# One core, grouped-query decode attention with a gated block: V of a step and K of the next in one 8 MiB transfer

## The chip, the core and the metric

The kernel runs on one core of a Trainium2 chip. TensorE (PE) multiplies matrices, VectorE (DVE) and ScalarE (ACT) work on tiles, SyncE (SP) issues the large transfers, and 16 DMA engines move them from the chip's main memory into the on-chip memory of 128 partitions. The metric is the device time of one execution in microseconds (us). Before the change it is 378.41 us, the median of 3 runs (378.18 to 378.69).

## What is computed

```python
def _A_ref(x, k_cache, v_cache, wq, wo):
    B, Sq, D = x.shape                     # 2, 1, 448
    Hq, Dh = 16, 256                       # Hkv = 8, Sk = 4096
    q = (x @ wq).reshape(B, Sq, Hq, Dh).transpose(0, 2, 1, 3)
    k = jnp.repeat(k_cache, 2, axis=1)
    v = jnp.repeat(v_cache, 2, axis=1)
    scores = jnp.einsum("bhqd,bhkd->bhqk", q, k) * (Dh ** -0.5)
    p = _softmax(scores, axis=-1)
    o = jnp.einsum("bhqk,bhkd->bhqd", p, v)
    return o.transpose(0, 2, 1, 3).reshape(B, Sq, Hq * Dh) @ wo
...
x = A_x
xn = _layernorm(x, axis=-1)
s = _A_ref(xn, A_k_cache, A_v_cache, A_wq, A_wo)
g = _silu(((xn @ w_gate) * (xn @ w_up)) @ w_down)      # F = 1792
return x + s * g
```

Everything is float32. For each of 2 batches and 8 key/value heads the caches hold 4096 positions by 256 values: 4 MiB of K and 4 MiB of V. With 16 such pairs and the weights, 158.5 MB are read once.

## The kernel before

**Steps.** The main loop (L279) runs over i = 0 to 13, one step for each pair of a key/value head g and a batch b (`g, b = divmod(i, 2)`); the last two steps, 14 and 15, stand behind it. A step has three parts. `scores(i)` (L195) multiplies q with K of the step: 16 matmuls of 128x512 in float32, which PE carries out as 32, into two PSUM banks, each followed by a maximum over the row on DVE (L206). `softmax` (L210) joins the maxima of the 128 partitions (a transposition on PE, L213, a maximum on DVE, L215, a matmul with a 1x1 one, L218, that turns the row back into a column, and a scaling, L219), takes exponentials on ACT (L224), transposes them on DVE (L226), and adds up and inverts the sums (L228 to L230). `values(i)` (L233) multiplies the exponentials with V: again 16 matmuls, 32 on PE, into the bank `o`, which ACT scales into `ob` (L286).

**Other work, placed by hand between the steps.** `query(0)` and `query(1)` (L151) make q of the first and the last four heads; `ffn_in` (L170) and `ffn_out` (L182) the gated block, behind steps 1 and 2; `combine` and `turn` (L240, L255) put the outputs of eight or six steps into the shape of a stationary operand; `project` (L261) multiplies them with parts of wo into the bank `wide`, `spread` (L162) brings `wide` into the bank `acc`, and `project_last` (L267) adds the last eight heads to `acc`. Two DVE operations (L338, L339) and a store (L340) follow.

**Order.** The order on every engine is that of the program. The large loads are listed by `plan` (L52) in the order in which they are to come, and `issue` (L55) gives the next ones to SP, which waits, where it must, until the buffer is free. All go through one pool, `ring`, of 5 buffers of 32 KB in each partition. The list is wq0, K0, V0, K1, V1, wg, wu, K2, V2, wd, K3, V3, and so on, with wq1 ahead of K6, wo0 ahead of K9, and at the end wo1, K14, K15, V14, V15 (in three pieces), wo2 (in four). The first five are issued at the start (L83). A K or V block is one transfer of 128 rows of 32 KB.

**The end.** Behind the loop come `combine` and `turn` of six steps, `project` of wo1, `spread`, then scores and softmax of step 14, scores and softmax of step 15 (L312 to L315), V of 14, half of V of 15, the joining of step 14, the other half of V of 15, and the last heads.

Of the kernel before, what the change touches and what calls it, by code (L numbers as in the profile page):

```python
# [8 lines left out]
F32 = mybir.dt.float32  # L9
# [4 lines left out]
B, D = 2, 448  # L14
HKV, REP, SK, DH = 8, 2, 4096, 256
# [5 lines left out]
FC = F // NT  # L21
KB = 16
ROW = 8192
SL = D // NT
NC = HKV * 4
EARLY = 16
LATE = 24
THIRD = [24, 25, 28, 29, 30, 31, 26, 27]
EPS = 1e-5

# [5 lines left out]
@with_exitstack  # L36
def gated_decode_block(ctx: ExitStack, tc: tile.TileContext, x, xo, kt, v, wq, wo, wg, wu, wd, out):
    nc = tc.nc
    ring = ctx.enter_context(tc.tile_pool(name="ring", bufs=5))
    const = ctx.enter_context(tc.tile_pool(name="const", bufs=1))  # L40
# [4 lines left out]
    def bank(name="s", bufs=3):  # L45
        return psum.tile([128, 512], F32, name=name, bufs=bufs)


    loaded = {}
    todo = []  # L50

    def plan(name, src, cuts=None):  # L52
        todo.append((name, src, cuts or [0, src.shape[1]]))

    def issue(n=1):  # L55
        for name, src, cuts in todo[:n]:
            t = loaded[name] = ring.tile([128, ROW], F32, name="ring", align_bytes=512)
            for lo, hi in zip(cuts, cuts[1:]):
                nc.sync.dma_start(t[:, lo:hi], src[:, lo:hi])  # L59
        del todo[:n]  # L60

    N = HKV * B
    LAST = N - B
    plan("wq0", wq[0])
    for i in range(LAST):
        if i == 2:
            plan("wg", wg)
            plan("wu", wu)
        if i == 3:
            plan("wd", wd)  # L70
        if i == 6:
            plan("wq1", wq[1])
        if i == 9:
            plan("wo0", wo[:, :EARLY * D])
        plan(f"k{i}", kt[i % B, i // B])
        plan(f"v{i}", v[i % B, i // B])
    plan("wo1", wo[:, EARLY * D:LATE * D])
    plan(f"k{LAST}", kt[0, HKV - 1])
    plan(f"k{LAST + 1}", kt[1, HKV - 1])
    plan(f"v{LAST}", v[0, HKV - 1])  # L80
    plan(f"v{LAST + 1}", v[1, HKV - 1], [0, 4096, 7168, 8192])
    plan("wo2", wo[:, LATE * D:], [0, 2 * D, 6 * D, 7 * D, 8 * D])
    issue(5)  # L83

# [76 lines left out]

    def spread(ps, dst, start, stop):  # L162

        t = work.tile([128, D], F32, name="h")
        nc.scalar.copy(t, ps[:, :D])
        for n in range(NT):
            nc.tensor.matmul(dst[W * n:W * (n + 1), :SL], add_tiles.rearrange("p b j -> p (b j)"),
                             t[:, n * SL:(n + 1) * SL], start=start, stop=stop)

    def ffn_in():  # L170
        pp = []
        for w in ("wg", "wu"):
            ps = bank()
            rows(ps, loaded[w], FC)
            pp.append(ps)
        g = work.tile([128, FC], F32, name="h")
        nc.scalar.copy(g, pp[0][:, :FC])
        h = work.tile([128, FC], F32, name="h")
        nc.vector.tensor_mul(h, pp[1][:, :FC], g)
        nc.vector.transpose(hT.rearrange("p i m -> p (i m)"), h)  # L180

    def ffn_out():  # L182
        ps = bank()
        for i in range(14):
# [25 lines left out]
    def softmax(ss, m):  # L210
        nc.vector.tensor_max(m[:, 2:3], m[:, 0:1], m[:, 1:2])  # L211
        sm = bank("sm", 1)
        nc.tensor.transpose(sm[:1, :128], m[:, 2:3], ident)  # L213
        mx = work.tile([1, NT, W], F32, name="mx")
        nc.vector.tensor_reduce(  # L215
            mx, sm[:1, None, :128].rearrange("p o (c j) -> p o j c", c=NT).to_broadcast([1, NT, W, NT]),
            axis=AX.X, op=OP.max)
        nc.tensor.matmul(sm[:, 128:129], mx.rearrange("p c j -> p (c j)"), one, start=True, stop=True)  # L218
        nc.vector.tensor_scalar(m[:, 3:4], sm[:, 128:129], -1.0 / 16, None, op0=OP.mult)  # L219
# [53 lines left out]
    query(0)  # L273
    issue()
    ob = work.tile([128, 8, 512], F32, name="ob", bufs=1)
    oT0 = const.tile([128, 4, 2, REP, W], F32)
    oT1 = const.tile([128, 3, 2, REP, W], F32)
    oT2 = const.tile([128, 1, 2, REP, W], F32)
    for i in range(LAST):  # L279
        g, b = divmod(i, B)  # L280
        ss = scores(i)
        issue()
        p = softmax(*ss)
        o = bank("o", 1)
        values(i, p[0], o)
        nc.scalar.activation(ob[:, b * 4 + g if g < 4 else b * 3 + g - 4], o, AF.Copy, scale=p[1])  # L286
# [92 lines left out]
```

## Time and profile before

| what | value |
|---|---|
| median of 3 runs | 378.41 us |
| the profiled execution | 378.55 us |
| its span | 376.4 us |
| PE, DVE, ACT busy | 222.5, 72.7, 39.8 us |
| bytes read | 158.54 MB |
| mean granted TensorE clock | 0.77 |

How to read it: the span runs from the first to the last instruction of the profiled execution, and the 2.15 us around it belong to the run's time as well. Busy time is the time in which an engine executes something; for PE, which works in a pipeline, it is rough. The profile's page lists the span in 40 slices, the DMA queues, the chain of work that ended last, groups of instructions (line, engine, operation, shapes and count, then busy us and mean ns, then the idle time ahead of them and what ended it) and the DMA issues with their sizes and the time from issue to landing. Windows give the busy time of each engine in a stretch (PE, PE's weight loads, DVE, ACT, GpSimd), then the granted clock, the DMA share and GB/s. Timeline rows give start and duration in us, engine, line, operation and count.

### The profile page before, as it was taken

What the parts mean: (1) busy time and instruction counts of PE and PEld (TensorE: products, weight loads), DVE (VectorE), ACT (ScalarE), POOL (GpSimd) and SP (SyncE); (2) the same over time, 40 slices, a digit from 0 to 9 for tenths busy, and PEclk for the clock granted to TensorE, in tenths of its full rate; (3) what the DMA queues carried; (4) which work ended last, traced back from release to release, by engine and by line L of the source; (5) the groups of instructions that cost most, each with busy time, mean ns of one, the idle gap of its engine ahead of it and who ended that gap; (6) DMA issues with size and microseconds to landing.
All of it is one profiled execution on the core that took longest, in us unless ns stands there. A gap on an engine that the chain in (4) does not pass through costs nothing.

```text
span 376.4 us, 3397 instructions
## 1 busy us (share of the span) xinstructions
PE 222.5 (59%) x1456; PEld 65.6 (17%) x1456; DVE 72.7 (19%) x176; ACT 39.8 (11%) x87; POOL 1.2 (0%) x7
## 2 busy tenths in 40 slices
PE   0665556566376566646566655664656475574775
PEld 0112111112122111101121111121112121111122
DVE  3013030121021402102121310222112210304211
ACT  1001011001202200200102110011101010111011
POOL 1000000000000000000000000000000000000000
PEclk9966869766965877687886978669686966699669
DMA  8999999999999999999999999999999999999993
GB/s 333 437 439 416 435 430 438 428 429 444 425 434 439 435 420 436 438 435 432 420 439 437 432 424 432 442 437 421 427 442 435 435 423 428 435 428 445 414 417 132
DMA packets 6530, 158.75 MB, mean 422 GB/s; under 512 B 754, under 2 KB 1012, under 8 KB 1396
## 3 DMA queue, kind: packets, MB, share of 16 engines
q1 hardware_dynamic: 6496, 158.54, 98.0%
q8 instruction: 11, 0.18, 0.2%
q14 instruction: 3, 0.02, 0.0%
q10 hardware_dynamic: 20, 0.01, 0.0%
HBM read 158.54 MB, written 0.00 MB: 421 GB/s over the span
## 4 chain that ended last, share of the span: by engine, by line
DMA 76%; PE 18%; DVE 3%; issue 1%; ACT 1%; SPq 0%; ACTq 0%
DMA ring<-kt 55%; DMA ring<-v 12%; DMA ring<-wd 9%; PE s L205 8%; PE o L237 6%; DVE pT L226 1%; PE wide L237 1%; PE s L186 1%; PE cb L246 1%; DVE m L206 1%; DVE mx L215 1%; PE sm L229 0%; PE acc L270 0%; SPq L59 0%; PE sm L218 0%
## 5 line engine op out<-in xcount | busy, mean ns | idle before, releaser
L205 PE MATMUL s<-ring,qT 128*32 128x512 f32 x512 | 82.0, 799 | 50.9 <-DMA ring<-kt 50.9
L237 PE MATMUL o<-ring,pT 128*32 128x512 f32 x480 | 82.4, 849 | 1.6 <-DMA ring<-v 1.6
L206 DVE TENSOR_REDUCE m<-s 128x1 f32<-128x512 f32 x32 | 22.1, 692 | 177.5 <-PE s L205 177.5
L224 ACT ACTIVATE p<-s,m 128x512 f32<-128x512 f32 x32 | 21.7, 682 | 197.1 <-DVE m L219 197.1
L205 PEld LDWEIGHTS s<-ring,qT 128*32 128x32 f32 x512 | 20.5, 141 | 110.3 <-issue 78.5
L229 PE MATMUL sm<-su,add_head 128*128 128x1 f32 x32 | 9.4, 362 | 42.4 <-DVE su L228 42.4
L237 PEld LDWEIGHTS o<-ring,pT 128*32 128x32 f32 x480 | 18.9, 149 | 51.5 <-issue 50.9
L226 DVE STREAM_TRANSPOSE pT<-p 128x512 f32<-128x512 f32 x32 | 22.1, 711 | 15.7 <-ACT p L224 15.7
L143 PE MATMUL s<-ring,xnT 128*32 128x512 f32 (+1 forms) x96 | 14.3, 746 | 12.3 <-DMA ring<-wq 7.7
L286 ACT ACTIVATE ob<-o,su 128x512 f32<-128x512 f32 x14 | 9.6, 687 | 98.8 <-PE o L237 98.8
L229 PEld LDWEIGHTS sm<-su,add_head 128*128 128x128 f32 x32 | 8.0, 311 | 43.8 <-DVE su L228 43.8
L213 PE MATMUL sm<-ident,m 128*1 128x128 f32 x16 | 4.3, 270 | 17.3 <-DVE m L211 17.3
L218 PE MATMUL sm<-one,mx 1*128 1x1 f32 x32 | 6.8, 279 | 12.3 <-DVE mx L215 12.3
L215 DVE TENSOR_REDUCE mx<-sm 1x128 f32<-1x512 f32 x16 | 10.9, 679 | 7.0 <-PE sm L213 7.0
L264 PE MATMUL wide<-ring,oT 128*32 128x448 f32 x48 | 6.6, 698 | 4.1 <-DMA ring<-wo 3.3
L218 PEld LDWEIGHTS sm<-one,mx 1*128 1x128 f32 x32 | 5.4, 211 | 15.8 <-DVE mx L215 15.8
L143 PEld LDWEIGHTS s<-ring,xnT 128*32 128x32 f32 x96 | 3.6, 132 | 21.0 <-issue 17.0
L213 PEld LDWEIGHTS sm<-ident,m 128*1 128x1 f32 x16 | 1.3, 79 | 32.4 <-issue 26.6
L256 DVE STREAM_TRANSPOSE oT<-cb 128x256 f32<-128x256 f32 (+2 forms) x6 | 1.9, 347 | 25.5 <-PE cb L246 25.5
L224 ACT ACTIVATION_READ_ACCUMULATOR p<-s,m 128x1 f32 x32 | 6.3, 196 | 0.0
L155 DVE STREAM_TRANSPOSE qT<-s 128x256 f32<-128x256 f32 x4 | 1.6, 428 | 21.6 <-PE s L146 21.6
L246 PE MATMUL cb<-ob,add_blocks 128*32 128x64 f32 (+2 forms) x64 | 4.2, 384 | 2.3 <-ACT ob L286 1.6
(57 smaller groups left out, 47.0 us busy)
## 6 DMA issues: line engine op xcount, KB each, us to landing
ring<-kt SPq DMA_DIRECT2D x16, 4096.0 KB, 40.4
ring<-v SPq DMA_DIRECT2D x15, 4096.0 KB, 41.8
ring<-wq SPq DMA_DIRECT2D x2, 3584.0 KB, 11.3
ring<-wo SPq DMA_DIRECT2D x1, 3584.0 KB, 40.7
ring<-wg SPq DMA_DIRECT2D x1, 3136.0 KB
ring<-wu SPq DMA_DIRECT2D x1, 3136.0 KB
ring<-wd SPq DMA_DIRECT2D x1, 3136.0 KB, 34.5
ring<-v SPq DMA_DIRECT2D x1, 2048.0 KB
```

What stands on the lines that cost most here:

```text
L143: nc.tensor.matmul(ps[W * c:W * (c + 1), :n], xnT[:, k, :], block(NT * k + c), start=k == 0, stop=False)
L205: nc.tensor.matmul(s[W * c:W * (c + 1), :], q[:, d], k[:, h, d, c, :], start=d == 0, stop=d == 1)
L206: nc.vector.tensor_reduce(m[:, h:h + 1], s, axis=AX.X, op=OP.max)
L215: nc.vector.tensor_reduce(mx, sm[:1, None, :128].rearrange("p o (c j) -> p o j c", c=NT).to_broadcast([1, NT, W, NT]), axis=AX.X, op=OP.max)
L218: nc.tensor.matmul(sm[:, 128:129], mx.rearrange("p c j -> p (c j)"), one, start=True, stop=True)
L224: nc.scalar.activation(p, ss[h], AF.Exp, bias=m[:, 3:4], scale=1.0 / 16, accum_out=su[:, h:h + 1])
L226: nc.vector.transpose(t.rearrange("p i m -> p (i m)"), p)
L229: nc.tensor.matmul(sm[:, 130:131], add_head.rearrange("p a r j -> p (a r j)"), su[:, 2:3], start=True, stop=True)
L237: nc.tensor.matmul(o[W * t:W * (t + 1), :], pT[h].rearrange("p i m -> p (i m)")[:, at:at + 2 * W:2], loaded[f"v{i}"][:, e * 512:(e + 1) * ...
L246: nc.tensor.matmul(cb[W * c:W * (c + 1), :n * 64], add_blocks[:, e].rearrange("p r j -> p (r j)"), src[:, :n, e, :, c, :], start=e == 0, s ...
L264: nc.tensor.matmul(wide[W * t:W * (t + 1), :D], heads(oT, i, first), loaded[name][:, (i - base) * D:(i - base + 1) * D], start=i < NT, sto ...
L286: nc.scalar.activation(ob[:, b * 4 + g if g < 4 else b * 3 + g - 4], o, AF.Copy, scale=p[1])
```

## The change

K of step 0 is loaded by itself (`first`); from then on V of step i and K of step i + 1 lie side by side in one array, `vk[i]`, with 64 KB a row, and are loaded as one transfer of 8 MiB. The pool `ring` has 2 buffers of 64 KB a partition instead of 5 of 32 KB. The weights wq0, wg, wu, wd, wq1, wo0, wo1 and wo2 go one after the other through a pool of their own, `slot`, with one buffer of 28 KB. K15 and V14 share a buffer, loaded in two pieces; V15 comes in three pieces, as before.

So the order of the work changes. Step i of the loop is now values(i), then scores(i + 1), then softmax of i + 1. The next 8 MiB can be issued when both V of i and K of i + 1 have been used. In steps 0 and 1 the issue stands behind `gate_in` and `up_in` (`late`), because the weights to come need the slot. `ffn_in` is split into these two, in steps 0 and 1. `softmax` is split into its first part and `over`, the adding up and inverting. The matmul with a one, L218, becomes a transposition. At the end come scores of 14 (in the loop), softmax of 14 without `over`, scores of 15, `over` of 14, `project` of wo1, softmax of 15, V of 14, `spread`, `over` of 15, and V of 15; what follows is as before.

```diff
@@ -34,9 +35,10 @@
 
 
 @with_exitstack
-def gated_decode_block(ctx: ExitStack, tc: tile.TileContext, x, xo, kt, v, wq, wo, wg, wu, wd, out):
+def gated_decode_block(ctx: ExitStack, tc: tile.TileContext, x, xo, first, vk, last0, last1, wq, wo, wg, wu, wd, out):
     nc = tc.nc
-    ring = ctx.enter_context(tc.tile_pool(name="ring", bufs=5))
+    ring = ctx.enter_context(tc.tile_pool(name="ring", bufs=2))
+    slot = ctx.enter_context(tc.tile_pool(name="slot", bufs=1))
     const = ctx.enter_context(tc.tile_pool(name="const", bufs=1))
     work = ctx.enter_context(tc.tile_pool(name="work", bufs=2))
     psum = ctx.enter_context(tc.tile_pool(name="psum", bufs=1, space=bass.MemoryType.PSUM))
@@ -46,41 +48,39 @@
         return psum.tile([128, 512], F32, name=name, bufs=bufs)
 
 
+
+    N = HKV * B
+    LAST = N - B
     loaded = {}
     todo = []
 
-    def plan(name, src, cuts=None):
-        todo.append((name, src, cuts or [0, src.shape[1]]))
-
     def issue(n=1):
-        for name, src, cuts in todo[:n]:
-            t = loaded[name] = ring.tile([128, ROW], F32, name="ring", align_bytes=512)
+        for names, src, cuts in todo[:n]:
+            if len(names) == 1 and names[0].startswith("w"):
+                t = loaded[names[0]] = slot.tile([128, PART], F32, name="slot", align_bytes=512)
+            else:
+                t = ring.tile([128, 2 * ROW], F32, name="ring", align_bytes=512)
+                for i, name in enumerate(names):
+                    loaded[name] = t[:, i * ROW:(i + 1) * ROW]
             for lo, hi in zip(cuts, cuts[1:]):
                 nc.sync.dma_start(t[:, lo:hi], src[:, lo:hi])
         del todo[:n]
 
-    N = HKV * B
-    LAST = N - B
+    def plan(names, src, cuts=None):
+        todo.append((names.split(), src, cuts or [0, src.shape[1]]))
+
     plan("wq0", wq[0])
+    plan("k0", first)
+    weights = {0: ("wg", wg), 1: ("wu", wu), 2: ("wd", wd), 4: ("wq1", wq[1]), 8: ("wo0", wo[:, :EARLY * D]),
+               12: ("wo1", wo[:, EARLY * D:LATE * D])}
     for i in range(LAST):
-        if i == 2:
-            plan("wg", wg)
-            plan("wu", wu)
-        if i == 3:
-            plan("wd", wd)
-        if i == 6:
-            plan("wq1", wq[1])
-        if i == 9:
-            plan("wo0", wo[:, :EARLY * D])
-        plan(f"k{i}", kt[i % B, i // B])
-        plan(f"v{i}", v[i % B, i // B])
-    plan("wo1", wo[:, EARLY * D:LATE * D])
-    plan(f"k{LAST}", kt[0, HKV - 1])
-    plan(f"k{LAST + 1}", kt[1, HKV - 1])
-    plan(f"v{LAST}", v[0, HKV - 1])
-    plan(f"v{LAST + 1}", v[1, HKV - 1], [0, 4096, 7168, 8192])
+        plan(f"v{i} k{i + 1}", vk[i])
+        if i in weights:
+            plan(*weights[i])
+    plan(f"k{LAST + 1} v{LAST}", last0, [0, ROW, 2 * ROW])
+    plan(f"v{LAST + 1}", last1, [0, 4096, 7168, 8192])
     plan("wo2", wo[:, LATE * D:], [0, 2 * D, 6 * D, 7 * D, 8 * D])
-    issue(5)
+    issue(3)
 
     x2 = const.tile([B, D], F32)
     nc.scalar.dma_start(x2, x)
@@ -159,24 +159,29 @@
     gate = const.tile([128, SL], F32)
     hT = const.tile([128, 14, W], F32)
 
-    def spread(ps, dst, start, stop):
-
+
+    def lift(ps):
         t = work.tile([128, D], F32, name="h")
         nc.scalar.copy(t, ps[:, :D])
+        return t
+
+    def spread(t, dst, start, stop):
         for n in range(NT):
             nc.tensor.matmul(dst[W * n:W * (n + 1), :SL], add_tiles.rearrange("p b j -> p (b j)"),
                              t[:, n * SL:(n + 1) * SL], start=start, stop=stop)
 
-    def ffn_in():
-        pp = []
-        for w in ("wg", "wu"):
-            ps = bank()
-            rows(ps, loaded[w], FC)
-            pp.append(ps)
-        g = work.tile([128, FC], F32, name="h")
-        nc.scalar.copy(g, pp[0][:, :FC])
+    def gate_in():
+        ps = bank()
+        rows(ps, loaded["wg"], FC)
+        g = const.tile([128, FC], F32)
+        nc.scalar.copy(g, ps[:, :FC])
+        return g
+
+    def up_in(g):
+        ps = bank()
+        rows(ps, loaded["wu"], FC)
         h = work.tile([128, FC], F32, name="h")
-        nc.vector.tensor_mul(h, pp[1][:, :FC], g)
+        nc.vector.tensor_mul(h, ps[:, :FC], g)
         nc.vector.transpose(hT.rearrange("p i m -> p (i m)"), h)
 
     def ffn_out():
@@ -186,7 +191,7 @@
             nc.tensor.matmul(ps[W * t:W * (t + 1), :D], hT[:, i], loaded["wd"][:, i * D:(i + 1) * D],
                              start=i < NT, stop=i >= 14 - NT)
         y = bank()
-        spread(ps, y, True, True)
+        spread(lift(ps), y, True, True)
         e = const.tile([128, SL], F32)
         nc.scalar.activation(e, y[:, :SL], AF.Sigmoid)
         nc.vector.tensor_mul(gate, y[:, :SL], e)
@@ -215,7 +220,7 @@
         nc.vector.tensor_reduce(
             mx, sm[:1, None, :128].rearrange("p o (c j) -> p o j c", c=NT).to_broadcast([1, NT, W, NT]),
             axis=AX.X, op=OP.max)
-        nc.tensor.matmul(sm[:, 128:129], mx.rearrange("p c j -> p (c j)"), one, start=True, stop=True)
+        nc.tensor.transpose(sm[:, 128:129], mx.rearrange("p c j -> p (c j)"), one)
         nc.vector.tensor_scalar(m[:, 3:4], sm[:, 128:129], -1.0 / 16, None, op0=OP.mult)
         su = work.tile([128, 4], F32, name="su")
         pT = []
@@ -225,6 +230,11 @@
             t = work.tile([128, KB, W], F32, name="pT", bufs=4)
             nc.vector.transpose(t.rearrange("p i m -> p (i m)"), p)
             pT.append(t)
+        return pT, su, sm
+
+    def over(p):
+
+        pT, su, sm = p
         nc.vector.tensor_add(su[:, 2:3], su[:, 0:1], su[:, 1:2])
         nc.tensor.matmul(sm[:, 130:131], add_head.rearrange("p a r j -> p (a r j)"), su[:, 2:3], start=True, stop=True)
         nc.vector.reciprocal(su[:, 3:4], sm[:, 130:131])
@@ -271,53 +281,61 @@
                              start=False, stop=i == THIRD[-1])
 
     query(0)
-    issue()
     ob = work.tile([128, 8, 512], F32, name="ob", bufs=1)
     oT0 = const.tile([128, 4, 2, REP, W], F32)
     oT1 = const.tile([128, 3, 2, REP, W], F32)
     oT2 = const.tile([128, 1, 2, REP, W], F32)
+    ss = scores(0)
+    issue(2)
+    p = over(softmax(*ss))
     for i in range(LAST):
         g, b = divmod(i, B)
-        ss = scores(i)
-        issue()
-        p = softmax(*ss)
         o = bank("o", 1)
         values(i, p[0], o)
+        ss = scores(i + 1)
+
+        n, late = 1 + (i + 1 in weights), i in weights and i + 1 in weights
+        if not late:
+            issue(n)
         nc.scalar.activation(ob[:, b * 4 + g if g < 4 else b * 3 + g - 4], o, AF.Copy, scale=p[1])
-        issue()
-        if i == 1:
-            ffn_in()
-            issue(2)
-        if i == 2:
-            ffn_out()
-            issue()
-        if i == 5:
-            query(1)
-            issue()
+        if i == LAST - 1:
+            cb = combine(ob, 6)
+        p = softmax(*ss)
+        if i < LAST - 1:
+            p = over(p)
         if i == 7:
             cb = combine(ob, 8)
             for n in range(B):
                 turn(oT0, cb[:, n * 256:(n + 1) * 256], 0, n, 4)
             ob = work.tile([128, 8, 512], F32, name="ob", bufs=1)
-        if i == 8:
-            project(oT0, 0, 0, EARLY, "wo0", 0)
-            issue()
-    cb = combine(ob, 6)
+        if i in weights:
+            if i == 0:
+                gt = gate_in()
+            if i == 1:
+                up_in(gt)
+            if i == 2:
+                ffn_out()
+            if i == 4:
+                query(1)
+            if i == 8:
+                project(oT0, 0, 0, EARLY, "wo0", 0)
+        if late:
+            issue(n)
+
     for n in range(B):
         turn(oT1, cb[:, n * 192:(n + 1) * 192], 0, n, 3)
+    ss = scores(LAST + 1)
+    ps = [over(p)]
     project(oT1, 4, EARLY, LATE, "wo1", EARLY)
     issue()
-    spread(wide, acc, True, False)
-    ps = []
-    for i in range(LAST, N):
-        ss = scores(i)
-        issue()
-        ps.append(softmax(*ss))
-
+    t = lift(wide)
+    p = softmax(*ss)
     o = bank("o", 1)
     values(LAST, ps[0][0], o)
+    spread(t, acc, True, False)
+    ps.append(over(p))
+
     nc.scalar.activation(ob[:, 6], o, AF.Copy, scale=ps[0][1])
-    issue()
     o = bank("wide", 1)
     values(LAST + 1, ps[1][0], o, 0, KB // 2)
     cb = combine(ob[:, 6:], 1)
...
+    vk = np.concatenate([v[:n], k[1:n + 1]], 2)
+    last = [np.concatenate([k[n + 1], v[n]], 1), c(v[n + 1])]
...
```

More of the change, by code (lines that the diff above doesn't have):

```diff
@@ L28 @@
 THIRD = [24, 25, 28, 29, 30, 31, 26, 27]
+PART = EARLY * D
 EPS = 1e-5
 @with_exitstack
-def gated_decode_block(ctx: ExitStack, tc: tile.TileContext, x, xo, kt, v, wq, wo, wg, wu, wd, out):
+def gated_decode_block(ctx: ExitStack, tc: tile.TileContext, x, xo, first, vk, last0, last1, wq, wo, wg, wu, wd, out):
     nc = tc.nc
-    ring = ctx.enter_context(tc.tile_pool(name="ring", bufs=5))
+    ring = ctx.enter_context(tc.tile_pool(name="ring", bufs=2))
+    slot = ctx.enter_context(tc.tile_pool(name="slot", bufs=1))
     const = ctx.enter_context(tc.tile_pool(name="const", bufs=1))
@@ L352 @@
     k = np.asarray(A_k_cache).reshape(B, HKV, NT, W, 2, KB, 2, 128)
-    kt = c(k.transpose(0, 1, 7, 4, 6, 2, 5, 3)).reshape(B, HKV, 128, ROW)
-    v = c(A_v_cache).reshape(B, HKV, 128, ROW)
+    k = k.transpose(1, 0, 7, 4, 6, 2, 5, 3).reshape(HKV * B, 128, ROW)
+    v = np.asarray(A_v_cache).reshape(B, HKV, 128, ROW).transpose(1, 0, 2, 3).reshape(HKV * B, 128, ROW)
+    n = HKV * B - B
+    first = c(k[0])
+    vk = np.concatenate([v[:n], k[1:n + 1]], 2)
+    last = [np.concatenate([k[n + 1], v[n]], 1), c(v[n + 1])]
     def folded(w, n):
@@ L370 @@
     nc = bacc.Bacc("TRN2", target_bir_lowering=False, num_devices=1, dynamic_dma_scratch_size=2048)
-    arrays = dict(x=x, xo=xo, kt=kt, v=v, wq=wq, wo=wo, wg=wg, wu=wu, wd=wd)
+    arrays = dict(x=x, xo=xo, first=first, vk=vk, last0=last[0], last1=last[1], wq=wq, wo=wo, wg=wg, wu=wu, wd=wd)
     args = [nc.dram_tensor(n, a.shape, mybir.dt.from_np(a.dtype), kind="ExternalInput").ap()
```

## The prediction

> **What bounds the kernel now.** I read the page from the slices down to the DMA issues, then windows over the steady part, then the end.
>
> ```profile
> span 376.4 us, 3397 instructions
> ...
> DMA  8999999999999999999999999999999999999993
> GB/s 333 437 439 416 435 430 438 428 429 444 425 434 439 435 420 436 438 435 432 420 439 437 432 424 432 442 437 421 427 442 435 435 423 428 435 428 445 414 417 132
> DMA packets 6530, 158.75 MB, mean 422 GB/s; under 512 B 754, under 2 KB 1012, under 8 KB 1396
> ...
> q1 hardware_dynamic: 6496, 158.54, 98.0%
> ```
>
> The DMA row is 9 in every slice but the first and the last: the 16 engines are busy for 98% of the span. Windows say whether "busy" has holes that a rounded digit hides:
>
> ```profile
> 60.00:200.00 140.00, 81.34 (x513) 23.60 (x505) 25.98 (x58) 16.04 (x35) 0.00 (x0) 0.76 1.00 433
> 200.00:330.00 130.00, 79.21 (x480) 23.06 (x484) 24.78 (x57) 12.80 (x30) 0.00 (x0) 0.75 1.00 433
> 250.00:300.00 50.00, 30.00 (x199) 8.56 (x191) 9.68 (x22) 4.95 (x11) 0.00 (x0) 0.81 1.01 435
> 300.00:335.00 35.00, 21.52 (x121) 6.26 (x121) 6.20 (x15) 4.26 (x10) 0.00 (x0) 0.71 0.99 428
> ```
>
> The last three columns are granted clock, DMA share and GB/s. The share is 1.00 over 270 us at 433 GB/s, and TensorE is busy for 60% of the same time. So the middle of the kernel is a queue of bytes that never runs dry: 158.54 MB at 433 GB/s are 366.1 us of the 376.4. What remains is the start, and the end behind the last byte. A change can gain only from more bytes per us, from those 10 us, or lose by letting the queue run dry.
>
> Who keeps it full? The issues and SP's own waits:
>
> ```profile
> ring<-kt SPq DMA_DIRECT2D x16, 4096.0 KB, 40.4
> ...
> SPq L59 <- PE o L237: 96.9, 14, 10.0
> ```
>
> A K block lands 40.4 us after its issue, while 4096 KB at 433 GB/s take 9.7 us: some 31 us of work lie ahead of it. SP waits for matmuls to give a buffer back (96.9 us for the V blocks alone, up to 10.0 at a time), and this costs nothing as long as three to four transfers lie behind.
>
> The end, as the timeline and short windows show it:
>
> ```profile
> 339.19 3.64 PE L205 MATMUL s<-ring,qT 128*32 128x512 f32 x32 [0.67 <-DMA ring<-kt]
> ...
> 348.84 6.49 PE L205 MATMUL s<-ring,qT 128*32 128x512 f32 x32 [0.34 <-DMA ring<-kt]
> ...
> 355.41 0.69 DVE L206 TENSOR_REDUCE m<-s 128x1 f32<-128x512 f32 x1 [2.16 <-PE s L205]
> ...
> 360.95 5.56 PE L237 MATMUL o<-ring,pT 128*32 128x512 f32 x32
> ...
> 370.24 0.69 ACT L326 ACTIVATE ob<-wide,su 128x512 f32<-128x512 f32 x1 [2.97 <-PE wide L237]
> ...
> 371.78 1.36 PE L270 MATMUL acc<-ring,oT 128*32 128x112 f32 x48 [0.18 <-DVE oT L256]
> 373.21 0.28 DVE L338 TENSOR_TENSOR r<-acc,gate 128x112 f32<-128x112 f32 x1 [1.48 <-PE acc L270]
> ```
> ```profile
> 370.00:371.00 1.00, 0.37 (x16) 0.13 (x8) 0.00 (x0) 0.69 (x1) 0.00 (x0) 1.00 0.35 133
> 371.00:372.00 1.00, 0.82 (x33) 0.58 (x37) 0.25 (x1) 0.00 (x0) 0.00 (x0) 1.00 0.10 38
> 372.00:376.40 4.40, 1.14 (x48) 0.90 (x40) 0.55 (x2) 0.00 (x0) 0.00 (x0) 0.85 0.01 2
> ```
>
> The transfers thin out from 370 on and end a little after 372. The last heads' matmuls start at 371.78, released by the transposition of the last output (oT L256), and end at 373.2. So bytes and compute end within about 0.7 us of each other; the 3.2 us from 373.2 to the end (two VectorE steps, the store) do not change.
>
> **The change, part by part.** The profiled execution took 378.55 us for its span of 376.4 (2.15 around it); the median of the runs is 378.41. I sum against 378.55 and take 0.14 off at the end.
>
> *Fewer, longer rows.* 14 pairs of 4096 KB (28 transfers, 3584 packets of 32 KB) become 14 transfers of 64 KB rows. They carry 117.4 MB, 271 us at 433 GB/s. No row of this trace shows a 64 KB row, so I bound it. Above: the best long window runs at 435; all of the 271 us at 435 instead of 433 gain 1.2 us, and at 435 instead of 432 (the lowest that rounds into such a mean) 1.9 us. Below: 300 to 335 runs at 428; if long rows ran like that, 271 x 5/433 = 3.1 us would be lost. Nothing speaks for a large gain, since the share is already 1.00: what can go is a fixed cost in each packet that the share counts as busy. I take 0.6 us gained, half of the first bound, as near to the 433 of both long windows as to the 435 of one.
>
> The Trainium skill, "DMA: Bandwidth & Descriptors", section Why small descriptors are slow, names a fixed cost of about 3 cycles a packet and 32 bytes of metadata; by it 112 fewer packets on each engine would save some tenths of a us, an estimate, and the sum would be about the same.
>
> *Instructions.* The joining of maxima (L218) becomes a transposition:
>
> ```profile
> L213 PE MATMUL sm<-ident,m 128*1 128x128 f32 x16 | 4.3, 270 | 17.3 <-DVE m L211 17.3
> L218 PE MATMUL sm<-one,mx 1*128 1x1 f32 x32 | 6.8, 279 | 12.3 <-DVE mx L215 12.3
> ```
>
> Matmul L218 takes two passes a step (x32 in 16 steps), the transposition L213 one (x16), so PE issues 16 matmuls less and a step's chain gets about 0.1 us shorter (6.8/16 less 4.3/16 is 0.16). It is off the path in the middle, where PE waits for transfers, and I count nothing for it. SP issues 14 transfers fewer, which it has time for now as well.
>
> *Depth.* This is where the change can lose. Five buffers become two of twice the size and a slot for weights. The next 8 MiB can be issued only when V of a step and K of the next are both consumed. From one landing to the next lie 19.4 us (8192 KB at 433). In these PE does V and K. Prices per block are:
>
> ```profile
> L205 PE MATMUL s<-ring,qT 128*32 128x512 f32 x512 | 82.0, 799 | 50.9 <-DMA ring<-kt 50.9
> L237 PE MATMUL o<-ring,pT 128*32 128x512 f32 x480 | 82.4, 849 | 1.6 <-DMA ring<-v 1.6
> ```
>
> 82.0/16 and 82.4/15 are 5.1 and 5.5 us, together 10.6; at the worst block of the end, 6.5 us each, 13.0. So the buffer comes free 10.6 to 13 us after the landing, and 6 to 9 us of the other transfer still lie in the queue, against the time from an issue to its bytes:
>
> ```profile
> 0.74 0.39 SPq L59 DMA_DIRECT2D ring<-wq  x1
> ...
> 0.00:2.00 2.00, 0.00 (x0) 0.00 (x0) 0.16 (x3) 0.00 (x0) 0.70 (x6) 1.00 0.61 145
> ```
>
> The first issue is at 0.74, and by 2.00 some 290 KB have moved: bytes come about 1 us after an issue. The softmax (355.41 to 360.95, 5.5 us) follows and is done 16 to 19 us after the landing, ahead of the next V. So in the plain steps the queue stays full, and the loss is nothing.
>
> *Weight steps.* In steps 0 and 1 SP waits for gate_in or up_in to free the slot, and the next 8 MiB are queued behind that wait on SP. For the worst case I take:
>
> ```profile
> 42.73 5.34 PE L205 MATMUL s<-ring,qT 128*32 128x512 f32 x32 [3.82 <-DMA ring<-kt]
> ...
> 67.20 4.07 PE L143 MATMUL s<-ring,xnT 128*32 128x448 f32 x24 [4.15 <-DMA ring<-wu]
> 71.20 0.98 PE L146 MATMUL s<-ring,xnT 64*32 64x448 f32 x8
> ```
>
> V0 and K1 land when K1 does now, 42.7. Values and scores take 10.6 to 13, softmax 5.5, the gate's rows 5.0: done at 64 to 66. In the queue then lie wg (3136 KB, 7.4 us) and V1/K2 (19.4), until 69.5. About 3 to 5 us are left; step 1 has the same spacing. Nothing is lost, but this is the narrowest place of the loop.
>
> *The end.* After the landing of V13/K14 the same bytes follow as after K14 now (K15, V14, V15 and wo2, 14080 KB, 33.3 us). But PE then has V13 and scores(14) to do, not scores(14) alone, so scores(15) starts later, and the interleaving has to win that back. The clock decides the price of each block, so its rows:
>
> ```profile
> 340.90:344.30 3.40, 2.19 (x21) 0.47 (x13) 1.61 (x4) 0.00 (x0) 0.00 (x0) 1.00 1.01 436
> 344.30:347.80 3.50, 0.38 (x2) 0.29 (x2) 2.12 (x5) 1.45 (x4) 0.00 (x0) 1.00 0.99 426
> 347.80:354.60 6.80, 6.34 (x30) 1.89 (x34) 0.93 (x4) 0.00 (x0) 0.00 (x0) 0.50 0.97 419
> 354.60:358.00 3.40, 1.37 (x11) 0.37 (x3) 1.64 (x4) 0.00 (x0) 0.00 (x0) 1.00 0.93 400
> 358.00:364.90 6.90, 4.47 (x22) 1.49 (x26) 1.64 (x5) 1.45 (x4) 0.00 (x0) 0.51 0.99 420
> ```
>
> Behind a window with 0.38 or 1.37 us of matmuls in 3.4 the granted clock is 0.5; behind one with 2.19, and behind the full 6.34, it is 1.00. So a pause halves the clock, and dense work brings it back: 32 matmuls take 3.64 us at 339 and 6.49 at 349. The Trainium skill, "TensorE: Matmul & The Clock Gate", Part 1, says this too: an idle window of about 3.4 us throttles, a busy one releases; the rows agree.
>
> In the new end PE has no pause as long as the one at 344. From the landing of V13/K14 at 338.6 (339.2 less the 0.6) I count, at full clock: two blocks 7.3, combine 1.5, the small steps of softmax on PE 1.6, scores(15) 3.6, last reduction, sum and its matmul 1.5, project 1.7, small steps 1.6 = 18.8, so V14 could start at 357.4. Its bytes come at 358. The first blocks follow a pause, so one half-clock window of 6.8 us is added, which costs 6.49 less 3.64 = 2.9 us: 360.3. The rows of combine, project and the small steps (343.92 to 345.54, 1.6):
>
> ```profile
> 333.49 1.50 PE L246 MATMUL cb<-ob,add_blocks 128*32 128x384 f32 x16 [0.82 <-ACT ob L286]
> ...
> 335.75 1.71 PE L264 MATMUL wide<-ring,oT 128*32 128x448 f32 x16 [0.77 <-DVE oT L256]
> ...
> 343.92 0.27 PE L213 MATMUL sm<-ident,m 128*1 128x128 f32 x1 [1.10 <-DVE m L211]
> ...
> 345.38 0.16 DVE L219 TENSOR_SCALAR m<-sm 128x1 f32<-128x1 f32 x1 [0.47 <-PE sm L218]
> ```
>
> V14 3.6, spread and sum 1.0, V15 3.6 (368.5; its last bytes come at 367.7, 4.2 ahead of wo2's), then the way from the copy to the last heads, 370.24 to 371.78, 1.5: 370.0, against 371.78 now. The last bytes come at about 372.5 - 0.6 = 371.9, and only 8 matmuls (0.25 us) wait for them: 372.2 against 373.2 now. So the bytes end it, and the end comes 1.0 us earlier: 0.6 of the rows, and 0.3 to 0.4 because compute is no longer the later one. I take 0.9.
>
> Sum: 378.55 - 0.9 = 377.65, against the median 377.5.
>
> **Rivals.** *A, forecast*: 377.5, own range 376.9 to 378.0. For it speaks the unbroken DMA share, against it that each step of it is small.
>
> *B, nothing per byte*: the long rows are moved as two of 32 KB, or the fixed cost per packet is nil. Only the 0.3 of the end stays: 378.1. The mean of 433 in both long windows, whatever mix of rows, speaks for it.
>
> *C, the end is compute*: PE gets a second half-clock window between V13 and V14. From 360.3 the start of V14 moves to 363.2, the last heads to 372.9, their end to 374.3 to 374.8 (1.4 us, more at half clock): 1.1 to 1.6 later than now, and at 5.1 to 5.5 us a block throughout up to 3 later. Place: PE between the landing of V13/K14 and V15. It decides from the point where V14 starts after 362. Price: 379.6 to 381, I name 380.0. For it: six blocks stand in a row where now pauses absorb delays; against it: windows over 2.1 us of 3.4 kept the clock.
>
> *D, the queue dries or the long rows are slower*: if gate_in ends after 68 instead of 64 to 66, each us later is lost once a weight step. Or 64 KB row pitch costs rate: 3.1 us by the 428 window, 381.5. For the first: SP's waits of up to 10 us; against: 3 us of room. The Trainium skill, "DMA: Bandwidth & Descriptors", section Latency and other measured facts, reports copies at large power-of-two row pitches as slower (207 GB/s at 512 KiB, 164 at 2 MiB, of 214). By that rule this pitch doubles in the wrong direction, but 64 KiB lies below its first entry; no run shown so far has that pitch.
>
> *E, more*: the rate reaches 435 throughout, 1.9 + 0.4 us: 376.1.
>
> **Numbers.** A 0.40, B 0.16, C 0.20, D 0.12, E 0.12. A measurement of this kernel can tell about 0.2% (0.76 us) from no change, so faster means below 377.65, slower above 379.17. A's range gives 0.28 faster and 0.12 same; with E faster is 0.40, with B same is 0.28, and C and D are 0.32 slower. The range runs from E's middle (376.3) to C's (380.4); D and the rest, under 0.2, are left out.
>
> **What would show it.** DMA share 1.00 between 20 and 367 us with no slice below 415, and packets down by some 1800 or more (only a few hundred: B's splitting). Windows over the middle above 433: the rows' gain; at 433: B; below 430: D. SP's waits for PE may grow: harmless while the share stays. In the end: clock 1.00 from about 345 on, and the last heads' matmuls waiting for wo rather than for oT: A; waiting for oT with a 0.5 window between 345 and 362: C. A hole behind a weight step at 60 to 100 us: D. I am wrong altogether if the queue runs dry in plain steps.

## The result and the profile after

The changed kernel takes 377.74 us (median of 16 runs, 377.46 to 378.23), the kernel before 378.45 us beside it (16 runs): ratio 0.9982, 95% interval 0.9974 to 0.9990. That is 0.7 us, 0.4 to 1.0 by the interval. Repeated later, the two gave 377.61 and 378.33, ratio 0.9981 (0.9972 to 0.9989). The forecast was 377.5, 0.9 us less than the median that it started from. The measured median lies inside the forecast's own range (376.9 to 378.0), 0.1 us above the 377.65 below which the prediction speaks of "faster" (chance 0.40; "same" had 0.28).

The page of the changed kernel, its DMA rows (40 slices of 9.4 us, then packets and the queue's share):

```profile
span 375.8 us, 3331 instructions
...
DMA  8999999998999999999999999999999999999993
GB/s 340 439 464 391 433 455 440 453 434 386 431 440 448 440 406 440 440 440 440 434 440 440 441 397 451 437 433 433 419 446 441 412 433 434 433 415 440 413 416 134
DMA packets 4514, 158.74 MB, mean 422 GB/s; under 512 B 531, under 2 KB 789, under 8 KB 1173
...
q1 hardware_dynamic: 4480, 158.54, 97.9%
q8 instruction: 11, 0.18, 0.2%
```

The row of nines is as it was. The queue has 4480 packets instead of 6496: 2016 less, of which 1792 are rows, since two rows of 32 KB have become one of 64 KB, and 224 are the closing packets of 14 transfers (16 each). Single slices swing more than before (386 to 464) because packets of 64 KB are counted whole in one slice.

Windows of the changed kernel over the middle (last columns: clock, DMA share, GB/s):

```profile
60.00:200.00 140.00, 78.36 (x521) 22.07 (x513) 23.75 (x54) 15.25 (x31) 0.00 (x0) 0.74 1.00 431
200.00:330.00 130.00, 68.21 (x459) 21.35 (x459) 26.97 (x62) 14.25 (x34) 0.00 (x0) 0.74 1.00 433
```

The share is 1.00 again. The rate does not show the gain: 0.5 us of 366 is 0.14%, less than the rounding and the coarse counting (with 32 KB rows in the same layout, run e13 below, these windows read 432 and 432). The weight steps, in the timeline:

```profile
60.89 0.96 PE L146 MATMUL s<-slot,xnT 64*32 64x448 f32 x8
61.91 0.33 SPq L66 DMA_DIRECT2D slot<-wu  x1
62.33 0.38 SPq L66 DMA_DIRECT2D ring<-vk  x1
...
68.74 2.79 PE L247 MATMUL o<-ring,pT 128*32 128x512 f32 x12 [6.89 <-DMA ring<-vk]
```

gate_in ends at 61.9, SP issues at once, and the other 8 MiB land at 68.7: 6.8 us of work were still in the queue. The end of the changed kernel:

```profile
338.04 6.52 PE L247 MATMUL o<-ring,pT 128*32 128x512 f32 x32 [10.36 <-DMA ring<-vk]
344.37 3.62 PE L210 MATMUL s<-ring,qT 128*32 128x512 f32 x32
...
350.40 3.64 PE L210 MATMUL s<-ring,qT 128*32 128x512 f32 x32
...
355.23 1.71 PE L274 MATMUL wide<-slot,oT 128*32 128x448 f32 x16
...
358.06 3.64 PE L247 MATMUL o<-ring,pT 128*32 128x512 f32 x32
...
366.03 2.27 PE L247 MATMUL wide<-ring,pT 128*32 128x512 f32 x16 [1.42 <-DMA ring<-last]
...
370.52 1.17 PE L280 MATMUL acc<-slot,oT 128*32 128x112 f32 x40 [0.81 <-DMA slot<-wo]
371.92 0.40 PE L280 MATMUL acc<-slot,oT 128*32 128x112 f32 x8 [0.23 <-DMA slot<-wo]
372.39 0.28 DVE L356 TENSOR_TENSOR r<-acc,gate 128x112 f32<-128x112 f32 x1 [2.55 <-PE acc L280]
```

PE begins V of 13 at half clock (6.52 us behind a pause of 10.36) and does every later block in 3.62 to 3.64. The second half of V15 waits for its own bytes, the last heads wait for wo, and no longer for the transposed output. Three windows of the same stretch show the clock, first behind the pause and then where PE works on:

```profile
338.00:341.00 3.00, 2.96 (x16) 0.90 (x20) 0.00 (x0) 0.00 (x0) 0.00 (x0) 0.50 0.94 404
...
354.80:358.20 3.40, 2.51 (x24) 1.06 (x28) 1.00 (x6) 0.53 (x1) 0.00 (x0) 1.00 0.94 400
...
365.00:368.40 3.40, 2.35 (x20) 0.62 (x24) 0.00 (x0) 0.05 (x1) 0.00 (x0) 1.00 1.01 413
```

From 344.5 to 372.3 no window of 3.4 us, wherever it is laid, has less than about 2 us of matmuls, and the granted clock is 1.00 in all of them.

### The profile page after: what moved, and what is told of

It reads as the page before. It is cut to its first block, busy times and chain, and to the rows that moved or that the text cites. A ratio compares the mean times of both kernels' runs of the same rounds, so it can differ in the third digit from the quotient of the medians.

```text
span 375.8 us, 3331 instructions
## 1 busy us (share of the span) xinstructions
PE 202.5 (54%) x1440; PEld 61.4 (16%) x1440; DVE 72.3 (19%) x176; ACT 39.8 (11%) x87; POOL 1.2 (0%) x7
## 3 DMA queue, kind: packets, MB, share of 16 engines
q1 hardware_dynamic: 4480, 158.54, 97.9%
## 4 chain that ended last, share of the span: by engine, by line
DMA 74%; PE 23%; DVE 1%; issue 1%; SPq 0%; ACT 0%; ACTq 0%
DMA ring<-vk 65%; PE o L247 11%; PE s L210 9%; DMA ring<-first 5%; DMA slot<-wo 4%; PE s L143 1%; SPq L66 0%; PE wide L274 0%; DVE m L211 0%; DVE mx L220 0%; DVE pT L231 0%; PE cb L256 0%; PE sm L239 0%; PE s L146 0%; PE sm L218 0%
## 5 line engine op out<-in xcount | busy, mean ns | idle before, releaser
L210 PE MATMUL s<-ring,qT 128*32 128x512 f32 x512 | 59.7, 607 | 3.9 <-DMA ring<-first 3.9
L231 DVE STREAM_TRANSPOSE pT<-p 128x512 f32<-128x512 f32 x32 | 22.1, 711 | 15.7 <-ACT p L229 15.7
L210 PEld LDWEIGHTS s<-ring,qT 128*32 128x32 f32 x512 | 17.6, 112 | 43.4 <-issue 39.3
L143 PE MATMUL s<-slot,xnT 128*32 128x512 f32 (+1 forms) x96 | 18.0, 913 | 5.5 <-DMA slot<-wq 5.5
L218 PE MATMUL sm<-ident,m 128*1 128x128 f32 x16 | 4.3, 269 | 15.2 <-DVE m L216 15.2
L223 PE MATMUL sm<-one,mx 1*128 1x1 f32 x16 | 3.5, 217 | 12.3 <-DVE mx L220 12.3
L274 PE MATMUL wide<-slot,oT 128*32 128x448 f32 x48 | 7.1, 743 | 0.0
L143 PEld LDWEIGHTS s<-slot,xnT 128*32 128x32 f32 x96 | 4.0, 161 | 15.1 <-issue 15.1
L256 PE MATMUL cb<-ob,add_blocks 128*32 128x64 f32 (+2 forms) x64 | 6.0, 498 | 0.4 <-ACT ob L344 0.4
L218 PEld LDWEIGHTS sm<-ident,m 128*1 128x1 f32 x16 | 1.3, 79 | 29.1 <-issue 25.0
L191 PE MATMUL s<-slot,hT 128*32 128x448 f32 x28 | 5.2, 861 | 0.0
L247 PE MATMUL wide<-ring,pT 128*32 128x512 f32 x32 | 4.2, 599 | 1.7 <-DMA ring<-last 1.7
L240 DVE RECIPROCAL su<-sm 128x1 f32<-128x1 f32 x16 | 2.7, 168 | 11.0 <-PE sm L239 11.0
## 6 DMA issues: line engine op xcount, KB each, us to landing
ring<-first SPq DMA_DIRECT2D x1, 4096.0 KB, 20.5
```

The source lines that it names most:

```text
L143: nc.tensor.matmul(ps[W * c:W * (c + 1), :n], xnT[:, k, :], block(NT * k + c), start=k == 0, stop=False)
L210: nc.tensor.matmul(s[W * c:W * (c + 1), :], q[:, d], k[:, h, d, c, :], start=d == 0, stop=d == 1)
L247: nc.tensor.matmul(o[W * t:W * (t + 1), :], pT[h].rearrange("p i m -> p (i m)")[:, at:at + 2 * W:2], loaded[f"v{i}"][:, e * 512:(e + 1) * ...
L256: nc.tensor.matmul(cb[W * c:W * (c + 1), :n * 64], add_blocks[:, e].rearrange("p r j -> p (r j)"), src[:, :n, e, :, c, :], start=e == 0, s ...
L274: nc.tensor.matmul(wide[W * t:W * (t + 1), :D], heads(oT, i, first), loaded[name][:, (i - base) * D:(i - base + 1) * D], start=i < NT, sto ...
```

## The experiments

The theory: about 0.5 us come from fewer packets, up to 0.3 from an end that waits for bytes alone, and nothing is lost in the loop. The rivals: the end brings all of it, or the rows do, or the transposed maxima have a part; and two buffers may already cost something in the loop. Each ratio is against the kernel before, run beside it on the same chip.

| kernel | median us | ratio to before | 95% interval |
|---|---|---|---|
| changed | 377.74 | 0.9982 | 0.9974 to 0.9990 |
| changed, again | 377.61 | 0.9981 | 0.9972 to 0.9989 |
| e1, two rows of 32 KB | 377.98 | 0.9992 | 0.9983 to 1.0000 |
| e13, the same again | 378.17 | 0.9998 | 0.9990 to 1.0007 |
| e2, 16 pieces of 4 KB | 385.71 | 1.0193 | 1.0179 to 1.0207 |
| e3, plain end | 386.97 | 1.0216 | 1.0189 to 1.0244 |
| e4, before with the new end | 378.23 | 0.9995 | 0.9986 to 1.0004 |
| e8, e4 with transposed maxima | 378.18 | 1.0000 | 0.9991 to 1.0009 |
| e5, half of PE's work in the loop | 376.46 | 0.9955 | 0.9941 to 0.9969 |
| e6 and e9, issue line moved | 377.77, 377.82 | 0.9990, 0.9983 | 0.9981 to 0.9999, 0.9973 to 0.9993 |
| e10, buffer held 5 us | 380.07 | 1.0042 | 1.0028 to 1.0057 |
| e11, buffer held to the next V | 452.82 | 1.1969 | 1.1947 to 1.1991 |

**The rows.** One edit puts the 32 KB rows back and leaves all else:

```diff
-        plan(f"v{i} k{i + 1}", vk[i])
+        plan(f"v{i} k{i + 1}", vk[i], [0, ROW, 2 * ROW])
```

> The changed kernel, but each of the 14 transfers of 8 MiB is issued as two of 4 MiB into the same buffer, so a row is 32 KB again (3584 packets instead of 1792); buffers, order and end as in the changed kernel. Theory (the gain of 0.7 us is some 0.5 of fewer packets and some 0.3 of an end that waits for bytes alone): 0.4 to 0.6 us slower than the changed kernel, about 378.2, and 0.3 us or less faster than the kernel before. Rival 1 (the end, or the transposed maxima, bring all of it): as the changed kernel, 377.7. Rival 2 (the rows bring all of it): as before, 378.45.

Measured 377.98; the intervals of this and of the changed kernel overlap, so it was run again beside it:

> The changed kernel itself once more, so that it stands beside the next one on the same chip: 377.7, 0.6 to 0.8 us faster than before.

> The changed kernel with two transfers of 32 KB rows in place of each of 64 KB rows, again, beside the changed kernel on the same chip. From the 4 KB rows a packet costs 8.0 us / 1680 = 4.8 ns on its engine; 112 packets of that are 0.53 us: 378.2 to 378.3 if that is all of the rows' share; 378.0 if the earlier median holds, which would leave about half of it.

Measured 377.61 and 378.17, 0.56 us apart, side by side. Over both pairs the ratio without the long rows is 0.9995 on average, with them 0.9982: some 0.5 us are the rows'.

The traces settle it more sharply than the medians. Each transfer leaves a completion record on each of the 16 engines. From the first record of wq0 to the first record of the last transfer, that is, on the engine that is ahead, pass 357.1 to 357.4 us in the four traces of the changed order (the changed kernel, e12, e6, e9) and 357.75 to 358.0 in five with 32 KB rows (e1 and e13 in the new layout, the kernel before, e4 and e8 in the old one). The means are 0.56 us apart, and the layout makes next to no difference. The cost per packet alone, made large:

```diff
+            if len(names) == 2 and len(cuts) == 2:
+                nc.sync.dma_start(t.rearrange("p (a c) -> p a c", a=PIECES),
+                                  src.rearrange("p (a c) -> p a c", a=PIECES)[:, :, :2 * ROW // PIECES])
+                continue
...
-    vk = np.concatenate([v[:n], k[1:n + 1]], 2)
+    vk = np.concatenate([v[:n], k[1:n + 1]], 2).reshape(n, 128, PIECES, 2 * ROW // PIECES)
+    vk = np.pad(vk, ((0, 0), (0, 0), (0, 0), (0, 64))).reshape(n, 128, -1)
```

> The changed kernel, but each row of 64 KB is read as 16 pieces of 4 KB that lie 256 bytes apart in main memory: 16 times the packets of the 14 transfers (28672 instead of 1792), the same bytes, the same number of issues. Theory (a fixed cost in each packet; 0.5 to 0.6 us for 112 packets on each of 16 engines would be about 5 ns each): 1680 more packets on each engine cost 7 to 9 us, time 385 to 387. Rival (packets have no cost of their own at these sizes, and the gain came from the end): within 0.5 us of 377.7.

(`PIECES` is 16.) Measured 385.71, 8.0 us more than the changed kernel, inside the range. Its page:

```profile
DMA packets 31393, 158.74 MB, mean 414 GB/s; under 512 B 530, under 2 KB 788, under 8 KB 29844
...
q1 hardware_dynamic: 31360, 158.54, 99.6%
```

26880 more packets, 1680 on each engine, are 8.0 us: 4.8 ns a packet. The 112 fewer that the change brings are 0.53 us by that, which agrees with the 0.5 measured directly. The completion records agree: on the engine that is ahead, an 8 MiB transfer follows the one before in 19.32 us with 64 KB rows and in 19.88 with 4 KB, 0.56 us for 120 more packets. The engines are no less busy with the short rows (99.6%): a share of busy time counts the fixed cost as work, and this time the windows show it, at 422 GB/s:

```profile
200.00:330.00 130.00, 70.71 (x480) 21.42 (x472) 25.92 (x58) 12.80 (x30) 0.00 (x0) 0.74 1.02 422
```

The pieces of this run lie 256 bytes apart, so its pitch in main memory differs too. e1 keeps the pitch of 64 KB, and there too the shorter rows are slower; but e1 has 14 more transfers as well, which e2 has not. Neither run alone separates row length from all else; the two together do, as they give about the same price. The Trainium skill ("DMA: Bandwidth & Descriptors", Latency and other measured facts) reports slower copies at large power-of-two row pitches, from 512 KiB on. No run here has such a pitch, and at 64 KB there is no such effect: e1 has that pitch with the old rows and is no slower than the kernel before.

**The end.** Undone in the changed kernel (joining, project and spread ahead of scores of 15; softmax whole):

```diff
...
-    ss = scores(LAST + 1)
-    ps = [over(p)]
     project(oT1, 4, EARLY, LATE, "wo1", EARLY)
     issue()
-    t = lift(wide)
-    p = softmax(*ss)
+    spread(lift(wide), acc, True, False)
+    ss = scores(LAST + 1)
+    ps = [p, over(softmax(*ss))]
     o = bank("o", 1)
     values(LAST, ps[0][0], o)
-    spread(t, acc, True, False)
-    ps.append(over(p))
```

> The changed kernel with the end one after the other: step 14 with its sums, joining, project, spread, then scores and softmax of 15, then V of 14. Theory (interleaving is what keeps the end bound by bytes in this layout, where V of 13 and scores of 14 come in one piece): scores of 15 start at about 358 instead of 350, and PE pauses in both softmaxes, so V of 14 starts at 367 to 370 instead of 358: 6 to 12 us slower than the changed kernel, 384 to 390. Rival (the end is given by the bytes of wo2 anyway): at most 0.5 us slower.

Measured 386.97 (five runs, 385.48 to 387.68), 9.2 us slower than the changed kernel. The timeline:

```profile
360.07 3.62 PE L210 MATMUL s<-ring,qT 128*32 128x512 f32 x32
...
369.13 5.67 PE L247 MATMUL o<-ring,pT 128*32 128x512 f32 x32
```

Scores of 15 start at 360 and V of 14 at 369, ten and eleven us later than with interleaving. So in this layout the end's order is a condition of the change: without it the result would be 8.5 us on the other side. The same end put into the kernel before, and then the transposition as well:

> The kernel before with the end of the change alone (scores of 15, project, softmax and V of 14 interleaved in the same order); transfers, five buffers and main loop as before. Theory (bytes and compute end within 0.7 us of each other in the kernel before): 0.2 to 0.4 us faster than before, about 378.1, with the last heads' matmuls waiting for wo and not for oT. Rival 1 (the end brings all of the change): 0.7 us faster. Rival 2 (rows alone): no change.

> The kernel before with both of the change's other parts: the end interleaved and the joined maxima transposed instead of multiplied by a one; transfers, five buffers and main loop as before. Theory (the rest of the gain is the rows): as the kernel before with the new end alone, 378.1 to 378.3, and 0.3 to 0.5 us slower than the changed kernel. Rival (transposition brings the rest): 377.7.

```profile
371.56 1.40 PE L276 MATMUL acc<-ring,oT 128*32 128x112 f32 x48 [0.91 <-DMA ring<-wo]
```

That row is of e4: the last heads now wait for wo, as expected. The medians are 0.2 us and 0.0 us below the kernel before, and both intervals hold 1. By the medians the end and the transposition bring 0.2 us at most in the old layout, and the transposition nothing that can be told.

**Depth.** Two runs were to issue later:

```diff
-        if not late:
-            issue(n)
         nc.scalar.activation(ob[:, b * 4 + g if g < 4 else b * 3 + g - 4], o, AF.Copy, scale=p[1])
...
+        if not late:
+            issue(n)
```

> The changed kernel with the issue of the next 8 MiB put behind the softmax of the step instead of ahead of it, some 5 us later in every plain step (SP waits for the joined maxima's and sums' matmuls too). Theory (6 to 9 us of the other transfer are left in the queue when a buffer comes free): no loss in the loop, 377.7 to 378.2. Rival (two buffers are at their limit, the room is used up): a gap of some us in each of the 12 plain steps, 20 us or more slower.

> The changed kernel with the issue of steps 2 to 12 put behind the V matmuls of the following step, so SP gives out the next 8 MiB only after the other buffer has landed and half of it has been used. This takes away the cover of the two buffers. Theory: from each landing to the next bytes pass one V block (3.6 to 6.5 us) and about 1 us of issue, in 11 steps: 55 to 85 us slower, 433 to 463. Rival (the queue has other work in reserve): much less than 50 us.

Measured 377.77 and 377.82: nothing, also where 55 to 85 us were expected. The expectation missed what the edit does. SP carries nothing but these transfers and the store, and it waits for the last readers of the buffer and not for what stands above the line in the program. In all three traces it issues the same 32 transfers in the same order, each within 1.7 us of the changed kernel's time. Both runs test nothing of depth; they are two more runs of the changed order. To hold a buffer, something must read it:

```diff
+    def hold(i):
+        nc.tensor.matmul(acc[:W, 128:128 + SL], add_tiles.rearrange("p b j -> p (b j)"), loaded[f"v{i}"][:, :SL],
+                         start=True, stop=True)
```

> The changed kernel, but in the 12 steps without a late issue a tiny matmul (32 x 112, into an unused part of a bank) reads V of the step once more behind the softmax's sums, so that the buffer really comes free some 5 us later; SP's order is as in the changed kernel. Theory (6 to 9 us of the other transfer are still queued when a buffer comes free): no loss or little, 377.7 to 378.5, with issues of vk some 14 to 16 us behind a landing. Rival (the room is used up): some us in each of 12 steps, 20 us or more slower.

Measured 380.07, 2.4 us slower than the changed kernel, where 0 to 0.8 had been expected and the rival said 20. The timeline of e10:

```profile
189.07 6.28 PE L247 MATMUL o<-ring,pT 128*32 128x512 f32 x32 [4.35 <-DMA ring<-vk]
...
204.23 0.58 PE L284 MATMUL acc<-ring,add_tiles 128*32 128x112 f32 x2
```

A landing at 189.1, the release at 204.8, 15.7 us later; PE finds the other transfer landed at 208.5. So some 3.7 us between a release and the other landing are no longer enough. In the changed kernel the release comes some 9 us behind a landing (189.35, and the issue at 198.62), which leaves 10, and the least that is left there is 6.4 (a weight step: issue at 89.29, landing at 95.69).

The completion records say where the 2.4 us go. On the engine that is ahead, transfers of 8 MiB follow each other in 19.3 us. In e10 four of them take longer, 19.9, 20.0, 20.5 and 19.6; together that is 2.6 us. They were issued 2.1, 1.9, 0.9 and 3.1 us before this engine finished the other transfer. In the other eight steps this engine has 4.4 us or more left, mostly because a weight transfer is queued as well, and nothing is lost. The least that the changed kernel leaves it is 4.5 us (the same weight step), without a loss. So what is needed lies between 3.1 and 4.4 us, counted on the engine that is ahead. Counted to the landing that PE sees there is no such line: 6.4 us were left in the last of the four steps, which lost 0.3 us, and in the changed kernel's weight step, which lost nothing.

> As the run with the tiny matmul, but it stands behind the V matmuls of the following step, for steps 2 to 12: a buffer comes free only after the other one has landed and its V has been used, so the cover is gone. Theory: the queue runs dry in 11 steps, each time for one V block (3.6 to 6.5 us) and about 1 to 2 us from the issue to the first bytes, less what the fast engines lose: 50 to 90 us slower, 428 to 468, with dips of the DMA row in every step. Rival (something else keeps the engines busy): less than 20 us.

```profile
DMA  9999999999649996493984999648498496965995
```

Measured 452.82, 75 us slower. The loss is not even: by the completion records it is 8 to 10 us in each of the eight steps that find no weight transfer in the queue, and 0 to 4 in the other three. A V block and the reading matmul are about 6 us of it (landing at 150.66, issue at 156.32). The rest is the start of the queue, and where the engines had drifted apart, the wait for the last of them. From such an issue to the first completion pass 21.1 to 21.3 us instead of the 19.3 of a full queue, so 1.8 to 2.0 us are lost between an issue and its bytes. Where the queue runs dry, each us is lost.

**PE's work.** Scores and V of steps 0 to 13 halved:

```diff
-            for d in range(2):
+            for d in range(2 if i >= LAST else 1):
...
         for e in range(lo, hi):
+            if i < LAST and NT <= e < KB - NT:
+                continue
```

> The changed kernel, but in steps 0 to 13 only half of the matmuls of scores and of V are done (one of two halves of the head's 256 values; half of the positions of V), so the output is not the reference's; all bytes are still moved, steps 14 and 15 are whole. Theory (the middle is bound by bytes, PE hides behind them): no loss of PE's 70 us shows as a gain of more than about 1 us; up to 1 us may come because PE reads some 900 instructions less (2880 to about 2000), so fewer of the 11 instruction transfers of 16 KB hold up a DMA engine: 376.8 to 377.7. Rival (releases by PE hold back issues in the loop): several us faster, 375 or less.

Measured 376.46, 1.3 us faster than the changed order (377.74, and 377.77 and 377.82 beside it in e6 and e9); a little more than the 1 us allowed, far from the rival's 375. PE is busy for 155.6 us instead of 202.5, and the end waits for wo as before. What differs on the DMA side is the kind below the main queue:

```profile
q1 hardware_dynamic: 4480, 158.54, 98.2%
q8 instruction: 8, 0.13, 0.1%
```

8 instruction transfers instead of 11. The completion records agree: from the first landing of wq0 to the last byte pass 359.25 us here, 360.68 in the changed kernel, and the last transfer's first and last engine lie 1.9 us apart instead of 3.3. On the engine that is ahead both take the same, 357.35 and 357.36 us: less work on PE does not make the queue of bytes any shorter, it only brings the engines that were behind closer.

## Why the prediction was right

**The bound** (a queue of bytes that never runs dry): right. PE's busy time fell by 20 us through the change, the time by 0.7, and halving the loop's matmuls (e5) gained 1.3 us, none of it on the engine that is ahead.

**Rows, 0.6 us**: right: 0.5 by the medians, 0.53 by the cost of a packet, 0.56 by the completion records. The mechanism, a fixed cost in each packet that the share counts as busy, is what the runs show. That the size fits is luck: it was taken as half of the gap between two windows, which could not have shown it and afterwards did not. That the rows stay whole (rival B's splitting) the packet count shows.

**Depth and weight steps, nothing lost**: right in the result, with some luck. gate_in ended at 61.9 where 64 to 66 were reckoned. Most of that is an earlier landing, 41.1 instead of 42.7: in the kernel before, the last engine finished K1 2.3 us behind the first, after an instruction transfer at 37.1. The rest is that scores ran at full clock (3.61 us). So the weight steps kept 6.4 us or more where 3 to 5 were forecast, and the plain steps 10 where 6 to 9 were. But what is needed was understated: e10 loses 2.4 us where the count of 1 us from issue to bytes had called the room safe. Two things were wrong in that count. The first packets begin 1.0 to 2.0 us after an issue into an empty queue (129.6 to 130.6 for one at 128.66 in e11), and most of them take 2.7 to 3.5 us instead of 2.4, so that 1.8 to 2.0 us are lost. And the 16 engines run dry one by one, the first some 2 us ahead of the last, so the room has to be counted on the first. With 3 us left to the landing, the low end of the forecast, a weight step would have been where e10 lost 1.1 us (3.4 us left, at 273).

**Transposition, nothing**: not refuted; e8 against e4 shows nothing.

**The end, 0.3 to 0.4 us**: the mechanism was right to a few tenths. V of 14 at 358.06 (357.4 to 360.3 forecast), scores of 15 at 350.4, the last heads behind wo, their end at 372.3 (372.2). Rival C, a second half-clock window, did not come; the clock was 1.00 from 344.5 on, and 345 was named. But its worth was set too high: 0.2 us by the medians (e4; e1 and e13 on average), not told from 0 by the intervals. If one term makes the difference between the 0.9 forecast and the 0.7 measured, it is this one; the interval of 0.4 to 1.0 holds both. What the end's order is worth in the new layout is another matter: 9.2 us (e3).

**What would show it**: packets and the last heads' waits did. Two signs failed: no slice below 415 (386 is lowest) and a middle above 433 GB/s. By the second, 431 and 433 spoke for rival B, wrongly. Both asked too much of slices in which a packet of 64 KB counts whole. Rivals D and E did not come.

So of 0.7 us some 0.5 are the rows, 0.2 or less the end. Not settled is how much of that 0.2 is real.

## What to carry to other kernels

When the DMA share is 1.00 throughout, what is left are the fixed costs inside it: count packets per engine, and measure their price with a run that has many more of them, because windows cannot show a tenth of a per cent. The completion records can: take the engine that is ahead, the one that was held up least. Fewer, larger buffers cost nothing here as long as each comes free with room to spare before the other lands, and the price is sharp where that ends; count that room on the first engine to finish. Moving an issue in the program moves nothing if its queue waits for readers: look at what SP waits for before calling a transfer early or late.

## What the runs showed of the hardware

A packet costs about 4.8 ns on its engine beside its bytes, from 4 KB to 64 KB (e2; e1 and e13 agree). A transfer issued into an empty queue comes 1.8 to 2.0 us later than one behind others (21.1 to 21.3 us from issue to the first completion of 8 MiB in e11, against 19.3). The 16 engines do not end together: 3.3 us lie between the first and the last on the final transfer of the changed kernel, and with 3 instruction transfers of 16 KB fewer (e5) only 1.9, with the end 1.3 us earlier. In the records of DMA packets, a data packet that meets such a transfer takes 1.7 us instead of 1.2 (32 KB, kernel before), and its engine stays behind from then on, by some 1.5 us. That these transfers are the cause of the spread is read from the times of both; no run changed them alone.
